# Denominators of the first 256 tokens by a TensorE product, sums of batch 0 for two heads at a time, masks from the identity, and new instruction orders

## The chip, the cores and the metric

One core of a Trainium2 chip runs the whole program. The metric is the device time of one execution in microseconds; a lower number is better. Profiles are of one execution, taken by the hardware profiler.

## The reference

The kernel computes linear attention on polynomial features, followed by a two-layer MLP. The sizes are batch 4, 4 heads, 1088 tokens, head width 32, sketch rank 8, and an MLP of width 128 to 2048 to 128 on 4352 tokens.

```python
def phi(x):
    a = np.einsum('rd,bhsd->bhsr', S1, x)
    b = np.einsum('rd,bhsd->bhsr', S2, x)
    return np.einsum('bhsi,bhsj->bhsij', a, b).reshape(*x.shape[:-1], r * r)
q_p, k_p = phi(q), phi(k)
kv  = np.einsum('bhsf,bhsd->bhfd', k_p, v)
z   = np.sum(k_p, axis=2)
num = np.einsum('bhsf,bhfd->bhsd', q_p, kv)
den = np.einsum('bhsf,bhf->bhs', q_p, z)[..., None] + 1e-06
attn = num / den
x = attn.transpose(0, 2, 1, 3).reshape(B * S, H * D)
h = x @ w_in
out = (h - np.tanh(h)) @ w_out
```

All inputs and outputs are float32.

## The kernel before, in words

The program is a list of operations, each with its engine, its reads and its writes. `ORDER` holds, written out, the order of the operations on each of the five engines; a small planner only walks this order, places waits, and puts filler matmuls (lines 503 and 504, a product of a zero tile with itself) where its own cost figures see TensorE idle, up to the first operation that writes PSUM bank 0. Every engine runs its list strictly in order, and SyncE issues nearly all transfers, also in order.

Per batch, the steps are these. VectorE transposes the raw keys (kT, lines 569 and 573) and queries (qT, line 739). TensorE projects the keys on both sketches (kproj, 582), and VectorE turns the result (kab, 590). The sum over tokens of the key features is a Gram matrix of the two projections (gram, 598); it is masked to its head blocks (zm, 603), multiplied with S2 (ufold, 606), and reduced over heads (uw, 609) to eight more columns of the query projection's weights, w4. The query projection (qproj, 751) then gives, per token and head, the projections a and b and a third vector, whose product with a is the denominator: qab (759), dm (778), den (781), reciprocal rden (784), and qa = a/den (787). The outer products of a and b are qp for the queries (661 or 797) and wk for the keys (629). The sums over tokens of wk times v (642 for batch 0, 711 later) give kv, and the product of kv with the transposed qp gives x directly (693 for batch 0, 820 later).

Batch 0 goes in parts, so that the MLP can begin: tiles 0 and 1 of 128 tokens each alone, then 2 and 3, then 4 to 8. In batch 0, qp is transposed on TensorE (676), copied to qpB (683), and multiplied with kvb, which holds kv of two heads in a block (kvs 648, fold0 651, kvb 530 with pmask). Later batches transpose qp on VectorE (qpT, 803).

The MLP runs in windows of 256 or 512 tokens: L1 (912) multiplies x by a column block of w_in, ScalarE takes the tanh (916), L2 (925) multiplies with w_out. The linear part h @ w_out is folded to one 128 by 128 matrix: w_in is turned (857, 862) and multiplied with w_out (869, wfold), and its product with x is line 897. The weights are cast to bf16 at lines 843 and 847. Results are transposed (osb, 931) and stored (938).

In PSUM, operations of different engines that touch one bank are ordered by waits, also two readers.

Of the kernel before, what the change touches and what calls it, by code (L numbers as in the profile page):

```python
# [52 lines left out]
    ),  # L53
    "scalar": (
# [4 lines left out]
    ),  # L59
    "vector": (  # L60
# [5 lines left out]
    ),  # L66
    "gpsimd": (
        "6 4 5 2 16 20 3 25 7 18 17 19 23 22 79 21 80 24 81 109 106 110 107 108 111 150 152 241 242 247 251 363 365 364 374 370 "
        "508 506 507 517 513 "
    ),  # L70
    "sync": (
# [22 lines left out]
class Program:  # L94
# [46 lines left out]
    def schedule(self):  # L141
# [10 lines left out]
        free = {e: 0 if e == "sync" else BEGIN for e in engines}  # L152
# [10 lines left out]
        while left:  # L163
# [58 lines left out]
            for k in o.kids:  # L222
                seen = o.end + SEEN[k.eng]
# [120 lines left out]
def bass_polysketch_attn__then__act_tanh_shrink_kernel(nc, q, k, v, S1, S2, moe_w_in, moe_w_out, out):  # L344
# [26 lines left out]
    e4 = sb("e4", [4, 4, 4, 8])  # L371
    hmask = sb("hmask", [128, 2])
    pmask = sb("pmask", [128, 2])
    mask = sb("mask", [128, H, R])
# [16 lines left out]
    kvb = sb("kvb", [128, 2, 2, D])  # L391
    qpB = sb("qpB", [128, NT, 2, 128])
# [44 lines left out]
    def load_small():  # L437
        for i, src in enumerate((S1, S2)):
            o = load("scalar", 1024, ("s_raw",), "s", -1000, lambda e, i=i, src=src: e.dma_start(
                out=s_raw[8 * i:8 * i + 8, :], in_=src[:, :]), True)  # L440
            o.lag = -950
# [4 lines left out]
    def load_rows(dst, src, name, b, cuts, prios, first=0):  # L446
        i = b % 2
        for x, (lo, hi) in enumerate(cuts):
            hi = min(hi, S)
            size = 512 * (hi - lo)  # L450
            o = P.op("sync", size / (360 if b else 280), lambda e, lo=lo, hi=hi: e.dma_start(
# [3 lines left out]
            o.lag = 2500 if b == 1 else 0 if b or first else 1100  # L455
            asked.append((o, size))

    def load_keys(prio):
# [9 lines left out]
        for x, (g0, g1, lo, hi) in enumerate(((0, 4, 0, 160), (0, 3, 160, 288), (3, 4, 160, 224))):  # L468
            size = 512 * (g1 - g0) * (hi - lo)
            o = load("sync", size, ("kraw0", min(x, 1)), f"k0{min(x, 1)}", prio, runs(g0, g1, lo, hi), x == 2, 280)  # L470
            if x == 2:
                asked.append((o, size))

    def load_v(b, prio):
        i = b % 2
        src = v[b].rearrange("h (j c) d -> j h c d", j=32)
        for g in range(4):
# [3 lines left out]
                in_=src[:, :, 9 * g:9 * g + n, :].rearrange("j h t d -> j h (t d)")), True, 230)  # L481
            o.lag = 2500 if b == 1 else 0 if b else 900
        asked.append((o, 128 * 128 * 34))

    def load_w_in(prio):
        for x in range(4):
            o = load("sync", 262144, ("w_in_f", x), f"wi{x}", prio, rate=390, fn=lambda e, x=x: e.dma_start(
                out=w_in_f[:, 512 * x:512 * x + 512], in_=moe_w_in[:, 512 * x:512 * x + 512]))

    def load_w_out(prio):  # L490
        for x in range(4):
            load("sync", 262144, ("w_out_f", x), f"wo{x}", prio, rate=300, fn=lambda e, x=x: e.dma_start(
# [8 lines left out]
    def constants():  # L501
# [7 lines left out]
        P.op("gpsimd", 240, lambda e: e.memset(e4[:, :, :, :], 0.0), w=[("e4",)], prio=-999)  # L509
        P.op("gpsimd", 400, select(e4[:, :, :, :], [[0, 4], [-1, 4], [0, 8]], 0), r=[("e4",)], w=[("e4",)], prio=-999)  # L510
        P.op("gpsimd", 240, lambda e: e.memset(e16[:, :, :], 0.0), w=[("e16",)], prio=-998)
        P.op("gpsimd", 400, select(e16[:, :, :], [[0, 16], [-1, 8]], -8), r=[("e16",)], w=[("e16",)], prio=-998)
        P.op("vector", 110, lambda e: e.memset(hmask[:, :], 0.0), w=[("hmask",)], prio=-1000)  # L513
# [3 lines left out]
        P.op("vector", 110, lambda e: e.memset(pmask[:, :], 0.0), w=[("pmask",)], prio=-998)  # L517
        for h in range(2):
            P.op("vector", 110, lambda e, h=h: e.memset(pmask[64 * h:64 * h + 64, h:h + 1], 1.0),
                 w=[("pmask",)], prio=-998)  # L520
        P.op("gpsimd", 240, lambda e: e.memset(dm[:, :, :, R:R + 1], 1e-6), w=[("dme",)], prio=-975)
        for i in range(2):
# [3 lines left out]
            P.op("gpsimd", 240, lambda e, i=i: e.memset(w4[i][:, 24:32], 0.0), w=[("w40", i)], prio=-978 + i)  # L526
# [5 lines left out]
    def sketch():  # L532
# [8 lines left out]
        for h in range(2):  # L541
            scaled(psk[:, :, h, :], ps[:, 5, 0:16].rearrange("p (a i) -> p a i", a=2), hmask[:, h:h + 1], 16,
                   [bank[5], ("hmask",)], [("psk", h)], -899.5, f"psk{h}")
# [3 lines left out]
    def folding():  # L547
        P.op("tensor", 60, lambda e: e.matmul(
            ps[:, 6, 0:32], e4[:, :, :, :].rearrange("p a b c -> p (a b c)"), e4[:, 0, :, :].rearrange("p b c -> p (b c)"),
            start=True, stop=True), r=[("e4",)], w=[bank[6]], prio=-898, mode="s", name="mask", ni=4)  # L550
# [3 lines left out]
        P.op("scalar", act(32), lambda e: e.copy(mask[:, :, :].rearrange("p h i -> p (h i)"), ps[:, 6, 0:32]),  # L554
             r=[bank[6]], w=[("mask",)], prio=-861, name="mask")
        for h in range(H):
            scaled(s2blk[:, h, :], ps[:, 6, 64:96], mask[:, h, 0:1], 32, [bank[6], ("mask",)], [("s2blk", h)], -850, f"s2blk{h}")
# [5 lines left out]
    def keys(b, T, kb, gb, gate=()):  # L563
# [31 lines left out]
        def gram(e):  # L595
# [6 lines left out]
        P.op("tensor", 300, gram, r=[("kab", i, t) for t in range(NT)], w=[bank[gb]], prio=T["gram"], mode="128x32", name=f"gram{b}", ni=36)  # L602
        P.op("vector", dve(32), lambda e: e.tensor_tensor(
            out=zm[i][:, :], in0=ps[:, gb, 0:32], in1=mask[:, :, :].rearrange("p h i -> p (h i)"), op=ALU.mult),
# [30 lines left out]
    def values_first(T, vb, tb, tiled):  # L635


        for m, (t0, t1) in enumerate(tiled):
            def tiles(e, t0=t0, t1=t1, m=m):
                for t in range(t0, t1):  # L640
                    for h in range(H):
                        ins = e.matmul(ps[32 * h:32 * h + 32, tb, 0:64], vx[0][:, h, t, :], wk[:, t, h, :, :],
# [422 lines left out]
```

## Time and profile before

| what | value |
|---|---|
| median of 3 runs | 109.08 us (108.99 to 109.91) |
| the profiled execution | 108.55 us, span 106.7 us |
| TensorE (PE) busy | 96.8 us, 91% of the span |
| ScalarE (ACT) busy | 78.4 us, 73% |
| VectorE (DVE) busy | 61.7 us, 58% |
| GpSimd (POOL) busy | 35.0 us, 33% |
| granted TensorE clock | 1.00 |
| first L1 matmul of the MLP | at 17.26 us |
| num of batch 1 (line 820) | at 39.78 us |

The span is from the first to the last instruction; the time of the execution has 1.85 us more around it. Busy shares are averages over stages with different limits, so they don't say what bounds a stage: in the opening no token can enter the MLP before batch 0's keys, values and first queries have gone through four engines, while at the end only the MLP is left. In timeline lines the columns are start, duration, engine, line, operation, output and inputs, shape and count; in square brackets stands the idle time before it and what ended it. PEld is TensorE's weight load.

### The profile page before, as it was taken

What the parts mean: (1) busy time and instruction counts of PE and PEld (TensorE: products, weight loads), DVE (VectorE), ACT (ScalarE), POOL (GpSimd) and SP (SyncE); (2) the same over time, 40 slices, a digit from 0 to 9 for tenths busy, and PEclk for the clock granted to TensorE, in tenths of its full rate; (3) what the DMA queues carried; (4) which work ended last, traced back from release to release, by engine and by line L of the source; (5) the groups of instructions that cost most, each with busy time, mean ns of one, the idle gap of its engine ahead of it and who ended that gap; (6) DMA issues with size and microseconds to landing.
All of it is one profiled execution on the core that took longest, in us unless ns stands there. A gap on an engine that the chain in (4) does not pass through costs nothing.

```text
span 106.7 us, 2954 instructions
## 1 busy us (share of the span) xinstructions
PE 96.8 (91%) x1246; PEld 50.5 (47%) x1256; DVE 61.7 (58%) x128; ACT 78.4 (73%) x107; POOL 35.0 (33%) x45
## 2 busy tenths in 40 slices
PE   6899985899999969999899999999999999999960
PEld 3357553784656424424544443544344434345540
DVE  2467962999899998689986365927650020200210
ACT  3350874775458974859998797989969999999930
POOL 5737017450491920493930049391000000000000
PEclk9999999999999999999999999999999999999999
DMA  2999999930798300799100410033002324024063
GB/s 38 298 220 289 313 320 259 238 82 0 247 201 233 57 3 0 242 208 262 25 0 7 75 22 0 6 52 47 0 12 37 55 34 68 0 36 62 6 98 49
DMA packets 26509, 11.21 MB, mean 105 GB/s; under 512 B 19072, under 2 KB 24320, under 8 KB 26496
## 3 DMA queue, kind: packets, MB, share of 16 engines
q1 hardware_dynamic: 25920, 10.95, 43.7%
q8 instruction: 10, 0.16, 0.7%
q10 hardware_dynamic: 576, 0.07, 0.4%
q14 instruction: 3, 0.02, 0.1%
HBM read 8.78 MB, written 2.23 MB: 103 GB/s over the span
## 4 chain that ended last, share of the span: by engine, by line
PE 64%; DMA 10%; DVE 9%; ACT 4%; POOL 4%; SPq 3%; issue 3%; POOLq 0%; DVEq 0%
PE ps L925 23%; PE ps L912 23%; DMA w_out_f<-in_moe_w_out_dram 6%; ACT tt L916 4%; DMA vx<-in_v_dram 4%; PE ps L820 4%; PE ps L897 3%; DVE qpT L803 3%; POOL w_out L847 2%; PE ps L751 2%; DVE qp L797 2%; PE ps L582 2%; DVE qab L759 1%; SPq L466 1%; SPq L479 1%
## 5 line engine op out<-in xcount | busy, mean ns | idle before, releaser
L916 ACT ACTIVATE tt<-ps 128x1024 bf16<-128x1024 f32 (+1 forms) x70 | 66.7, 998 | 10.4 <-PE ps L912 8.5
L912 PE MATMUL ps<-xT,w_in 128*128 128x512 bf16 (+1 forms) x154 | 40.9, 346 | 1.6 <-issue 0.8
L925 PE MATMUL ps<-tt,w_out 128*128 128x512 bf16 (+1 forms) x157 | 39.9, 347 | 0.2 <-issue 0.2
L629 POOL TENSOR_TENSOR wk<-kab 128x768 f32<-128x768 f32 (+2 forms) x11 | 15.7, 1425 | 22.3 <-DVE kab L590 21.8
L925 PEld LDWEIGHTS ps<-tt,w_out 128*128 128x128 bf16 x160 | 15.4, 99 | 13.9 <-issue 2.2
L912 PEld LDWEIGHTS ps<-xT,w_in 128*128 128x128 bf16 x160 | 14.3, 97 | 16.0 <-ACT tt L916 4.9
L931 DVE STREAM_TRANSPOSE osb<-ps 128x512 f32<-128x512 f32 (+1 forms) x10 | 6.3, 634 | 22.6 <-PE ps L925 22.6
L797 POOL TENSOR_TENSOR qp<-qa,qab 128x768 f32<-128x768 f32 x6 | 10.3, 1710 | 6.2 <-DVE qa L787 5.9
L803 DVE STREAM_TRANSPOSE qpT<-qp 128x768 f32<-128x768 f32 x9 | 8.4, 959 | 3.1 <-POOL qp L797 3.1
L759 DVE STREAM_TRANSPOSE qab<-ps 128x576 f32<-128x576 f32 (+2 forms) x10 | 6.0, 642 | 3.7 <-PE ps L751 3.7
L739 DVE STREAM_TRANSPOSE qT<-qraw 128x576 f32<-128x576 f32 (+2 forms) x9 | 5.8, 653 | 0.0
L820 PE MATMUL ps<-qpT,kvw 32*32 32x288 f32 (+1 forms) x192 | 4.6, 399 | 0.8 <-DVE qpT L803 0.8
L503 PE MATMUL ps<-wz 128*128 128x512 bf16 x8 | 4.3, 583 | 1.0 <-DVE hmask L513 1.0
L590 DVE STREAM_TRANSPOSE kab<-ps 128x576 f32<-128x576 f32 (+2 forms) x5 | 3.2, 661 | 2.1 <-PE ps L582 2.1
L569 DVE STREAM_TRANSPOSE kT<-kraw 128x576 f32<-128x576 f32 x6 | 4.4, 751 | 0.0
L847 POOL CAST w_out<-w_out_f 128x512 bf16<-128x512 f32 x4 | 2.5, 615 | 5.6 <-DMA w_out_f<-in_moe_w_out_dram 5.2
L830 ACT CAST xT<-ps 128x256 bf16<-128x256 f32 x6 | 2.0, 377 | 3.0 <-PE ps L820 3.0
L797 DVE TENSOR_TENSOR qp<-qa,qab 128x768 f32<-128x768 f32 x3 | 4.2, 1411 | 0.0
L862 ACT COPY w_inT<-ps 128x512 bf16<-128x512 bf16 x4 | 2.3, 586 | 2.3 <-PE ps L857 2.2
L820 PEld LDWEIGHTS ps<-qpT,kvw 32*32 32x32 f32 x192 | 2.4, 103 | 2.8 <-DVE qpT L803 1.2
L711 PEld LDWEIGHTS ps<-wk,vx 128*32 128x32 f32 x216 | 3.2, 110 | 1.2 <-issue 1.2
L843 ACT CAST w_in<-w_in_f 128x512 bf16<-128x512 f32 x2 | 1.2, 618 | 3.3 <-DMA w_in_f<-in_moe_w_in_dram 3.3
(90 smaller groups left out, 94.5 us busy)
## 6 DMA issues: line engine op xcount, KB each, us to landing
vx<-in_v_dram SPq DMA_DIRECT2D x12, 144.0 KB, 4.0
qraw<-in_q_dram SPq DMA_DIRECT2D x4, 288.0 KB, 6.2
w_in_f<-in_moe_w_in_dram SPq DMA_DIRECT2D x4, 256.0 KB, 5.5
w_out_f<-in_moe_w_out_dram SPq DMA_DIRECT2D x4, 256.0 KB, 6.7
out_dram<-osb SPq DMA_DIRECT2D x16, 64.0 KB, 2.0
kraw<-in_k_dram SPq DMA_DIRECT2D x3, 288.0 KB, 5.5
kraw<-in_k_dram SPq DMA_DIRECT2D x3, 256.0 KB, 5.9
qraw<-in_q_dram SPq DMA_DIRECT2D x3, 256.0 KB, 5.5
```

The lines of the kernel that those rows point to most:

```text
L569: P.op("vector", dve(hi - lo), lambda e, lo=lo, hi=hi: e.transpose(out=kT[:, lo:hi], in_=kraw[i][:, lo:hi]), r=cells("kraw", i, lo, min(hi ...
L629: P.op(eng, dve(cols) if eng == "vector" else pool2(cols), lambda e, t0=t0, t1=t1, ap=ap, m=m, ka0=ka0: e.tensor_tensor(out=wk[:, t0:t1, : ...
L739: P.op("vector", dve(hi - lo), lambda e: e.transpose(out=qT[i][:, lo:hi], in_=qraw[i][:, lo:hi]), r=cells("qraw", i, lo, hi), w=cells("qT" ...
L759: P.op("vector", dve(2 * n), lambda e, h=h: e.transpose(out=qab[:, t0:t1, h:h + 2, :].rearrange("p t h x -> p h t x"), in_=ps[:, qb + h:qb ...
L797: P.op(eng, dve(cols) if eng == "vector" else pool2(cols), lambda e, p0=p0, p1=p1, w=w: e.tensor_tensor(out=qp[:, p0:p1, :, :, :].rearrang ...
L803: P.op("vector", dve(cols), lambda e, p0=p0, p1=p1: e.transpose(out=qpT[:, p0:p1, :, :, :].rearrange("p t h y j -> p (t h y j)"), in_=qp[: ...
L820: ins = e.matmul(ps[32 * h:32 * h + 32, nb[g], 0:32 * n], kvw[i][32 * g:32 * g + 32, y, 32 * h:32 * h + 32], qpT[32 * g:32 * g + 32, t0:t0 ...
L847: P.op("gpsimd", 600, lambda e, x=x: e.tensor_copy(w_out[:, 4 * x:4 * x + 4, :], w_out_f[:, 4 * x:4 * x + 4, :]), r=[("w_out_f", x)], w=[( ...
L912: P.op("tensor", pe(n), lambda e, jb=jb + y, y=y, hb=hb: e.matmul(hb[:, n * y:n * y + n], w_in[:, 128 * jb:128 * jb + 128], xT[:, f0:f0 + ...
L916: P.op("scalar", act(q * n), lambda e, un=un, hb=hb, q=q: e.activation(out=tt[:, un, 0:q * n], in_=hb[:, 0:q * n], func=AF.Tanh, scale=-1. ...
L925: P.op("tensor", pe(n), lambda e, jb=jb, un=un, y=y: e.matmul(acc[:, 0:n], w_out[:, jb, :], tt[:, un, n * y:n * y + n], start=(not f0 and ...
L931: P.op("vector", dve(n), lambda e: e.transpose(out=osb[u][:, 0:n], in_=acc[:, 0:n]), r=[ka], w=[("osb", u)], prio=slot0, name=f"osb{w}")
```

## The change

What it does:

- The first two tiles (256 tokens) no longer go through dm, den, rden and qa. Their query projection uses only the plain sketches (w4[1]). The Gram matrix is spread on VectorE (`zx`) and multiplied with the head mask on TensorE (`zfold`), which gives `zden`, a weight that puts each head's denominator on all 32 of the head's output channels. One product with qpB (`zq`) gives the denominators of 256 tokens; ScalarE adds 1e-6 (`dsum`), VectorE takes the reciprocal (`drec`) and multiplies (`x0`).
- The sums of batch 0 multiply two heads at once (128 features against 64 value columns, `pairs`), and the diagonal blocks are copied straight to `kvb`; fold0 and pmask go.
- The mask of head blocks is copied from the identity (`same`) and reduced (`mask`), where before it was a product of `e4` with itself.
- `ORDER` is new for all engines, and the planner's figures of transfers are other ones. One more key product (tile 5) goes to GpSimd.

```diff
+        for g in range(4):
+            P.op("vector", 110, lambda e, g=g: e.tensor_copy(
+                same[32 * g:32 * g + 32, :, :].rearrange("p h i -> p (h i)"), ident[32 * g:32 * g + 32, 32 * g:32 * g + 32]),
...
+        P.op("vector", 110, lambda e: e.tensor_reduce(out=mask[:, :], in_=same[:, :, :], axis=AX.X, op=ALU.add),
...
+            P.op("vector", dve(256), lambda e: e.tensor_tensor(
+                out=zx[:, :, :, :, :].rearrange("p x y i j -> p (x y) i j"),
+                in0=ps[:, gb, 0:32].rearrange("p (h i) -> p h i", i=R)[:, :, :, None].to_broadcast([128, H, R, R]),
+                in1=same[:, :, None, :].to_broadcast([128, H, R, R]), op=ALU.mult),
...
+            def spread(e):
+                for x in range(2):
+                    ins = e.matmul(ps[:, gb, 128 + 64 * x:192 + 64 * x], zx[:, x, :, :, :].rearrange("p y i j -> p (y i j)"),
+                                   mask[:, 2 * x:2 * x + 2, None].to_broadcast([128, 2, D]), start=True, stop=True)
...
+            P.op("scalar", act(128), lambda e: e.copy(
+                zden[:, :, :, :].rearrange("p x y d -> p (x y d)"), ps[:, gb, 128:256]), ...
...
-                        ins = e.matmul(ps[32 * h:32 * h + 32, tb, 0:64], vx[0][:, h, t, :], wk[:, t, h, :, :],
-                                       start=(t == tiled[0][0]), stop=(t == tiled[-1][1] - 1), tile_position=(0, 32 * h))
...
+                if not m:
+                    e.matmul(ps[:, tb, 0:128], wz[:, :], wz[:, :], start=True, stop=False)
+                for t in range(t0, t1):
+                    for x in range(2):
+                        ins = e.matmul(ps[:, tb, 64 * x:64 * x + 64], wk[:, t, 2 * x:2 * x + 2, :, :].rearrange("p h i j -> p (h i j)"),
+                                       vx[0][:, 2 * x:2 * x + 2, t, :], start=False, stop=(t == split[-1][1] - 1 and x == 1))
...
+            P.op("scalar", act(64), lambda e, y=y: e.copy(
+                kvb[64 * y:64 * y + 64, :, y, :], ps[64 * y:64 * y + 64, tb, 0:128].rearrange("p (x y d) -> p x y d", x=2, y=2)[:, :, y, :]),
...
+    def first_pair(t0, T, qb, ab, tb, db, nb, engs):
...
+            P.op("vector", dve(2 * n), lambda e, h=h, x=x: e.transpose(
+                out=qsb[:, u, x, :, :].rearrange("p (t h) f -> p h t f", h=2),
...
+            P.op("scalar", act(32), lambda e, x=x, near=near: e.copy(near, qsb[:, u, x, :, 0:R]),
...
+            P.op("vector", dve(256), lambda e, x=x, near=near: e.tensor_tensor(
+                out=qq[:, x, :, :].rearrange("p t f -> p (t f)").rearrange("p (m i j) -> p m i j", i=R, j=R),
...
+            P.op("tensor", 500, product(zden, db), r=[("zden",)] + ready, w=[bank[db]], prio=T["den"], mode="128x64", name=f"zq.{t0}", ni=8)
+            P.op("scalar", act(256), lambda e: e.activation(out=dsum[:, u, :], in_=ps[:, db, 0:256], func=AF.Copy, bias=1e-6),
...
+            P.op("vector", dve(256), lambda e: e.reciprocal(drec[:, u, :], dsum[:, u, :]), r=[("dsum", u)], w=[("drec", u)], prio=T["den"], name=f"drec{u}")
+            P.op("tensor", 500, product(kvb, nb), r=[("kvb", 0), ("kvb", 1)] + ready, w=[bank[nb]], prio=T["num"], mode="128x64", name=f"num0.{t0}", ni=8)
+            P.op("vector", dve(256), lambda e: e.tensor_tensor(
+                out=xT[:, 128 * t0:128 * t0 + 256], in0=ps[:, nb, 0:256], in1=drec[:, u, :], op=ALU.mult),
...
-    key_products(0, opening, [(0, 2, "gpsimd"), (2, 4, "gpsimd"), (4, 5, "gpsimd")] + [(t, t + 1, "vector") for t in range(5, 9)], 1)
+    key_products(0, opening, [(0, 2, "gpsimd"), (2, 4, "gpsimd"), (4, 5, "gpsimd"), (5, 6, "gpsimd")] + [(t, t + 1, "vector") for t in range(6, 9)], 1)
+    values_first(opening, 3, [(0, 2), (2, 4), (4, 5), (6, 7), (5, 6), (7, 9)])
+    casts(("scalar", "scalar", "gpsimd", "gpsimd"), ())
+    rest = first_pair(0, first, 4, (4, 6), (5, 7), 4, 6, ("scalar", "scalar"))
+    queries(0, 2, 4, then, 4)
+    rest()
```

The orders of the opening in the changed program, read from the built program, with its own line numbers:

- TensorE: fills (4 of 512 columns, 3 of 128), S product (541), fills (512, 512, 128), S2 product (554), kproj of tiles 5 to 8 and 0 to 4 (583), qproj of the first pair (688), gram (599), w_in turn 0, zfold (613), turns of qp (711), ufold (624), qproj of tiles 2 and 3 (830), sums of tiles 0 to 6 (662, 14 products), zq (728), sums of tiles 7 and 8 (4 products), turns of qp of tiles 2 and 3 (755), w_in turn 1, num0 (728), num of tiles 2 and 3 (772), w_in turn 2, three L1 (988), qproj of tiles 4 to 8, ... No fills follow the S2 product.
- VectorE: constants, the two kT, kab of tiles 5 to 8, qT, kab of tiles 0 to 4, two qsb (698), zx (605), two qp (704), qT, zm (620), wk of tile 6 (647), uw (627), wk of tiles 7 and 8, qab of tiles 2 and 3 (838), dm, den, rden, qa, two qp, qT, drec (737), x0 (739), qab of tiles 4 to 8, ...
- ScalarE: psk, s2blk, w4, cast of w_in 0, two qn (702), w_inT 0, zden (618), copy of keys, two qpB, cast of w_in 1, dsum (735), two kvb (669), qpB of tiles 2 and 3, w_inT 1, x of tiles 2 and 3, w_inT 2, tanh, ...
- GpSimd: constants, wk of tile 5, wk of tiles 0 and 1, memsets, wk of tiles 2 and 3, wk of tile 4, casts of w_in 2, w_out 0, w_out 1, w_in 3, w_out 2, w_out 3, ... (before: w_out 1, w_in 2, w_out 2, w_in 3, w_out 0, w_out 3).
- SyncE: keys (the smaller half first), q, w_in 0, v, q, three v, w_out 0, w_in 1, q, w_in 2, w_out 1, w_in 3, w_out 2, w_out 3; then the loads of batches 1 to 3 and the stores interleaved. Two of batch 1's four v loads stand behind the first load of batch 2, which waits for the last x of batch 0, and two of batch 2's four v loads stand behind the first load of batch 3, which waits for x of batch 1.

More of the change, by code (lines that the diff above doesn't have):

```diff
@@ L151, in schedule @@
         head = dict.fromkeys(engines, 0)
-        free = {e: 0 if e == "sync" else BEGIN for e in engines}
+        free = {e: BEGIN for e in engines}
         avail = {e: [] for e in engines}
@@ L222, in schedule @@
             for k in o.kids:
-                seen = o.end + SEEN[k.eng]
+                seen = o.end + SEEN[k.eng] + (300 if dma and k.eng == "gpsimd" else 0)
                 if k.eng == e and not dma:
@@ L370, in bass_polysketch_attn__then__act_tanh_shrink_kernel @@
     e16 = sb("e16", [16, 16, 8])
-    e4 = sb("e4", [4, 4, 4, 8])
     hmask = sb("hmask", [128, 2])
-    pmask = sb("pmask", [128, 2])
-    mask = sb("mask", [128, H, R])
+    same = sb("same", [128, H, R])
+    mask = sb("mask", [128, H])
     s_raw = sb("s_raw", [16, D])
@@ L391, in bass_polysketch_attn__then__act_tanh_shrink_kernel @@
     kvb = sb("kvb", [128, 2, 2, D])
+    zx = sb("zx", [128, 2, 2, R, R])
+    zden = sb("zden", [128, 2, 2, D])
+    dsum = sb("dsum", [128, 1, 256])
+    drec = sb("drec", [128, 1, 256])
+    qsb = sb("qsb", [128, 1, 2, H, 4 * R])
     qpB = sb("qpB", [128, NT, 2, 128])
@@ L454, in load_rows @@
                 after=gated(size))
-            o.lag = 2500 if b == 1 else 0 if b or first else 1100
+            o.lag = 1500 if b == 1 else 300
             asked.append((o, size))
@@ L516, in constants @@
                  w=[("hmask",)], prio=-1000)
[L517 to L520, printed above, removed]
+        P.op("gpsimd", 240, lambda e: e.memset(kvb[:, :, :, :], 0.0), w=[("kvb", 0), ("kvb", 1)], prio=-976)
         P.op("gpsimd", 240, lambda e: e.memset(dm[:, :, :, R:R + 1], 1e-6), w=[("dme",)], prio=-975)
@@ L659, in products_first @@
-    def products_first(T, t, eng, near=None, sb0=None):
-        qf = qa[:, t, :, :] if near is None else near
+                    for x in range(2):
+                        ins = e.matmul(ps[:, tb, 64 * x:64 * x + 64], wk[:, t, 2 * x:2 * x + 2, :, :].rearrange("p h i j -> p (h i j)"),
+                                       vx[0][:, 2 * x:2 * x + 2, t, :], start=False, stop=(t == split[-1][1] - 1 and x == 1))
+                return ins
+            P.op("tensor", 230 * (t1 - t0), pairs, r=[("wz",), ("vx", 0), ("vx0", 0)] + [("wk", t) for t in range(t0, t1)],
+                 w=[bank[tb]], prio=T["sums"] - 0.5 + m * T["sumstep"], mode="s", name=f"pairs.{t0}", ni=8 * (t1 - t0))
@@ L779, in denominators @@
             out=flat(dm)[:, :, 0:R], in0=flat(qab)[:, :, 0:R], in1=flat(qab)[:, :, 2 * R:3 * R], op=ALU.mult),
-            r=[("qab", t) for t in ts], w=[("dm", t) for t in ts], prio=T["den"], after=gate, name=f"dm{b}.{t0}", two=True)
+            r=[("qab", t) for t in ts], w=[("dm", t) for t in ts], prio=T["den"], name=f"dm{b}.{t0}", two=True)
         P.op("vector", dve(8 * m), lambda e: e.tensor_reduce(
@@ L785, in denominators @@
              r=[("den", t) for t in ts], w=[("rden", t) for t in ts], prio=T["den"], name=f"rden{b}.{t0}")
-        spot = flat(qa) if near is None else ps[:, near, 0:8 * m].rearrange("p (m i) -> p m i", i=R)
         P.op("vector", dve(8 * m), lambda e: e.tensor_tensor(
-            out=spot, in0=flat(qab)[:, :, 0:R], in1=flat2(rden)[:, :, None].to_broadcast([128, m, R]), op=ALU.mult),
-            r=[("qab", t) for t in ts] + [("rden", t) for t in ts], w=[("qa", t) for t in ts] + ([] if near is None else [bank[near]]),
-            prio=T["den"], name=f"qa{b}.{t0}", two=near is None)
-        return {} if near is None else {t: spot[:, 4 * (t - t0):4 * (t - t0) + 4, :] for t in ts}
+            out=flat(qa), in0=flat(qab)[:, :, 0:R], in1=flat2(rden)[:, :, None].to_broadcast([128, m, R]), op=ALU.mult),
+            r=[("qab", t) for t in ts] + [("rden", t) for t in ts], w=[("qa", t) for t in ts],
+            prio=T["den"], name=f"qa{b}.{t0}", two=True)
     def products(T, split, b):
@@ L963, in bass_polysketch_attn__then__act_tanh_shrink_kernel @@
                    sums=-850, sumstep=0.1, kvs=-872, kvb=-871)
-    keys(0, opening, ((1, 2), (3, 4)), 7)
+    keys(0, opening, ((1, 2), (3, 4)), 2)
     q_turn(0, 0, -891)
@@ L967, in bass_polysketch_attn__then__act_tanh_shrink_kernel @@
     first = dict(qproj=-892, qab=-892, den=-879, qp=-870, qpT=-869, num=-830, x=-829)
[L968 to L976 removed]
+    then = dict(qproj=-880, qab=-870, den=-820, qp=-819, qpT=0.1, num=2.6, x=-800)
+    key_products(0, opening, [(0, 2, "gpsimd"), (2, 4, "gpsimd"), (4, 5, "gpsimd"), (5, 6, "gpsimd")] + [(t, t + 1, "vector") for t in range(6, 9)], 1)
[4 more added lines that the diff above has]
+    rest()
     denominators(0, 2, 4, then)
[L978 to L979 removed]
     for x in range(4):
[L981 removed]
+        linear_turn((0.6, 0.7, 2.1, 2.2)[x], 0, x, "scalar")
     for t in range(2, 4):
         products_first(then, t, "vector")
[L984 to L986 removed]
+    numerators_first(then, [(2, 4, 5, "scalar")], 7, "scalar")
+    q_turn(0, 2, -800)
     second = dict(qproj=3.1, qab=-798, den=-795, qp=-774, qpT=-773, num=-772, x=-771)
```

127 lines of the change are left out of this document (75 added, 52 removed), and 52 rows, old and new, of the table ORDER.

## The prediction

> **What bounds the kernel now.** I read the chain of waits first, then the windows of busy time, then the timeline of the opening. The chain, in its stretch from 30 to 41 us:
>
> ```profile
> 30.88 1.46 DVE qab L759 x2
> ...
> 34.62 2.06 DVE qp L797
> 36.70 0.98 DVE qpT L803
> ...
> 37.98 1.75 DVE qpT L803 x2
> 39.78 1.55 PE ps L820 x50
> ```
>
> Until the numerators of batch 1 (num1, L820) start at 39.78, the tokens of batch 1 don't exist, and TensorE and ScalarE run out of windows. The chain before that is a VectorE chain. The windows (columns PE, PEld, DVE, ACT, POOL) show how full VectorE is there:
>
> ```profile
> 18.43:39.73 21.30, 19.92 (x268) 12.67 (x270) 20.37 (x38) 15.26 (x18) 10.22 (x8) 1.00 0.56 135
> 80.00:103.00 23.00, 22.87 (x119) 10.99 (x118) 2.23 (x4) 21.74 (x24) 0.00 (x0) 1.00 0.28 43
> ```
>
> VectorE works 20.37 of the 21.30 us from 18.43 to num1; afterwards the MLP fills TensorE and ScalarE. So the end is "start of that VectorE stretch, plus its work, plus a fixed rest". The stretch starts with qab of tiles 4 to 8 (L759). How it gets to 18.43 stands in the timeline:
>
> ```profile
> 15.77 0.27 ACT L699 CAST xT<-ps 128x128 bf16<-128x128 f32 x1
> 16.28 0.62 POOL L843 CAST w_in<-w_in_f 128x512 bf16<-128x512 f32 x1 [0.16 <-POOL w_out L847]
> 17.04 0.38 PE L857 MATMUL ps<-identb,w_in 128*128 128x128 bf16 x4 [0.99 <-POOL w_in L843]
> 17.26 0.49 PE L912 MATMUL ps<-xT,w_in 128*128 128x256 bf16 x3
> 18.43 0.91 DVE L759 STREAM_TRANSPOSE qab<-ps 128x320 f32<-128x320 f32 x2 [1.90 <-PE ps L751]
> 19.37 0.69 DVE L778 TENSOR_TENSOR dm<-qab 128x160 f32<-128x160 f32 x1
> ```
>
> The first x is whole at 16.04; a turn of w_in, held by a cast on GpSimd that itself stood behind a cast of w_out, keeps TensorE to 17.0; L1 starts at 17.26, and qab follows 1.17 us later. VectorE had idled 1.90 us for it. I therefore walk the changed opening to its first L1 and carry the shift to the end.
>
> **The change, part by part.** Prices come from these rows (first the reciprocal at three sizes, then TensorE):
>
> ```profile
> L784 DVE RECIPROCAL rden<-den 128x8 f32<-128x8 f32 x2 | 0.4, 194 | 0.0
> L784 DVE RECIPROCAL rden<-den 128x20 f32<-128x20 f32 x1 | 0.3, 278 | 0.0
> L784 DVE RECIPROCAL rden<-den 128x36 f32<-128x36 f32 x3 | 1.1, 378 | 0.1
> ...
> 11.76 0.30 PEld L651 LDWEIGHTS ps<-ident,kvs 128*128 128x128 f32 x2 [0.30 <-ACT kvs L648]
> 9.91 1.23 PE L642 MATMUL ps<-wk,vx 128*32 128x64 f32 x72
> 8.80 0.58 PE L503 MATMUL ps<-wz 128*128 128x512 bf16 x1
> 11.07 0.39 PE L503 MATMUL ps<-wz 128*128 128x512 bf16 x1
> ```
>
> *Head.* S lands as before (its product at 4.36). Behind it the new order has fills of 512, 512 and 128 columns instead of two of 128: a 512 goes every 0.40 us there (7.80 to 8.20), so +0.6, and kproj starts at 6.1 instead of 5.51. With the smaller half of the keys first, kab comes at 6.85 (6.40 before), then qT 0.40 and the second kab 0.52: 8.2.
>
> *First pair.* qproj now needs no folded sketch (w4[1], not w4[0]) and lies under the second kab. On VectorE follow: two qsb of 128 elements, 0.30 each (428 ns at 256 and 496 at 320 give 1 ns an element); zx 0.40 and two qp 0.40 each, as the 256-element products from PSUM; qT 0.40: from 8.35 to 10.55. qn, w_inT, zden and the copy of the keys (0.17 to 0.59 each) run on ScalarE beside this; zfold is two fp32 products of the kind of ufold (0.58), about 1.0 us, so zden ends at 10.7, and zm, which the bank makes wait for zden, ends at 10.9. ufold 0.6, uw: 11.8. Only now can the second qproj go (12.0 to 12.4), and behind it in TensorE's queue stand the sums of batch 0, which waited for nothing else (GpSimd's key products end near 11.7).
>
> *Sums.* Before, 36 tile products of 32 columns took 1.23 us (L642). Now 18 products load 128x128 fp32 weights in two passes each. The fold's two loads (L651: 188 ns each, 0.30 together) start 0.11 apart, the transposes of qp go every 0.13: I take 2 x 0.112 = 0.224 us a product, 4.0 us in all. Bounds: 0.07 (the tile price, 1.23/18) and 0.43 (ufold at 8.4 us: two loads of 337 ns, 0.215 apart). Fourteen of them stand ahead of zq: 12.5 + 3.1 = 15.65, zq 0.55 (L693 with 256 columns), dsum 0.38 on ScalarE: 16.6. ScalarE's w_in cast ahead of dsum waits for a transfer that I place near 12 (2.2 MB asked for up to it, against 2.4 MB landed by 12.9 before): 4 us of cover.
>
> *Reciprocal.* Before, one took 8 to 36 elements a partition. Now drec takes 256 in one instruction. The three rows give (378 - 194)/28 = 6.6 ns an element: 0.19 + 248 x 0.0066 = 1.83 us. Lower bound: 0.42, an ordinary 256-element operation; upper 1.9 (7.0 ns, the first two rows). I take 1.83, since three sizes lie on one line. VectorE reaches it at about 15.7 (wk, qab, dm to qa, two qp, qT: 3.9 us from 11.8) and waits for dsum: 16.6 to 18.45. The rest of the sums, four turns, a w_in turn and num0 (0.9 + 0.5 + 0.4 + 0.55) end at 18.4, beside it. x0 0.42: 18.9, first L1 at 18.95 instead of 17.26, +1.7.
>
> [...]
>
> *What is given back.* The casts are reordered by landing and end near 18.0 rather than 19.90; dm at 19.37 took 689 ns beside them, where 64 elements take 222 and 288 alone 460, so about 330: -0.36. VectorE's waits for TensorE later in the stretch (0.30 before zm, 0.23 before qab of batch 1) shrink when VectorE is the later one: I take half, -0.25. The VectorE list from qab to num1 is otherwise the same 38 instructions. The constants (e4, pmask gone, same and mask new) lie before 4 us, where VectorE idled 2.3 us for the keys; without that cover they cost 0.5. The masks' product and fold0 with its two kvb activations leave TensorE and ScalarE where both had idle time: nothing.
>
> *SP.* Loads and outputs are interleaved now. Two of batch 1's four v transfers stand behind a batch 2 load that waits for batch 0's last x (26 us); at up to 6.7 us to landing they arrive near 33, and sums1 is 0.85 us of MLP work later in TensorE's order than its 32.80: no cost, up to 1 if the queue is full. Batch 2's are a rival below.
>
> **Sum.** +1.7 - 0.36 - 0.25 = +1.1 us. The profiled execution took 108.55 (span 106.7 and 1.85 around it), 109.65 then; the median of the runs is 109.08, 0.53 higher, so 110.2.
>
> **Rivals.** (1) *Sums at the tile price*, chance 0.17: TensorE hides the loads, drec starts at 15.7 and x0 ends at 17.95; L1 at 18.0, +0.74 - 0.61: 109.2. For it: L642 does the same multiplications in 1.23. Against: L651.
> (2) *Faster*, 0.13: the same, and drec is an ordinary operation of 0.42. x0 then ends at 16.55, L1 at 16.6: -0.66 - 0.36, and up to 0.6 more if S lands earlier, so that the fills cost nothing: 107.9. It decides if drec lasts under 0.6 us. Against: the three L784 rows.
> (3) *TensorE stays slow*, 0.15: the 512-column fill took 0.58 up to 8.80 and 0.39 at 11.07, after fills that closed every gap from 6.65 on. The new order has no fill after the S2 product. If TensorE meets the sums at the slow price, ten instead of nineteen products fit into the 4.2 us that it needed before to speed up (4.95 to 9.2): zq 1.95 later, 112.1. The profile's granted clock stays 1.00 in both states. [...]
> (4) *Late v*, 0.05: batch 2's last two v transfers are issued after batch 1's x (42 us), the last as eighth; eight took 4.6 us, landing 3.6 to 6.7: 50 to 53 against sums2 at 51.47. From 5.2 us to landing on it stalls TensorE, on average by 1: 111.2.
>
> **Numbers.** Forecast 0.50, its own range 109.2 to 111.3. About 1% is what a measurement can tell here. Slower by more: 0.30 of the forecast, all of (3) and (4), 0.01 of (1): 0.51. Within 1%: 0.20, 0.13 of (1) and 0.03 of (2): 0.36. Faster: 0.10 and 0.03: 0.13. The range, 108.0 to 112.2, takes in (1), (3), (4) and the upper part of (2).
>
> **What would show it.** Right: L662 lasting 4 us with 0.22 between products, L737 at 1.8 us, first L1 near 18.9, num1 (L896) near 40.9. Wrong: L737 under 0.6; sums within 1.5 us; L1 before 17.3; or num1 that doesn't move with L1, which would mean that VectorE didn't bound the stretch.

## The result, and the profile after

The changed kernel takes 116.15 us (median of 4 runs, 115.22 to 117.39) against 109.06 (108.99 to 109.91, 4 runs of the kernel before): 1.0622 times as long, interval 1.0551 to 1.0692. The prediction had 110.2, at most 112.2. Its profiled execution took 116.43 us with a span of 114.1; before it was 108.55 and 106.7. So 7.9 us are to be found in one pair of traces. Here and below a time is the median of all runs of a kernel, while a ratio compares only the runs within 1.5% of each kernel's fastest one, so the two need not agree to the last digit.

The chain of waits of the kernel after (start, duration, engine, tile, line):

```profile
12.19 5.98 PE ps L662 x28
18.17 1.05 PE ps L728 x4
...
24.85 0.64 PE ps L988 x3
...
26.18 0.93 DVE qab L838 x2
...
46.92 1.61 PE ps L896 x50
...
53.88 5.19 DMA vx<-in_v_dram
```

First L1 (L988; 24.64 in the timeline below) starts 7.38 later than the 17.26 of before, the copy of the queries' projections (qab) starts at 26.18 instead of 18.43 (+7.75), the numerators of batch 1 (num1, L896) at 46.92 instead of 39.78 (+7.14), and the span ends 7.4 later. All of the loss lies ahead of the first L1, and the chain there is TensorE. Its largest piece is L662, the pair sums: 28 passes, that is 14 products, in 5.98 us. In the trace the passes start 0.213 us apart, two a product: 0.43 where the prediction took 0.224. The timeline shows the stretch:

```profile
11.99 6.18 PE L662 MATMUL ps<-vx,wk 128*128 128x64 f32 x28
18.10 1.12 PE L728 MATMUL ps<-qpB,zden 128*64 128x256 f32 x4
19.15 1.97 PE L662 MATMUL ps<-vx,wk 128*128 128x64 f32 x8
19.27 0.38 ACT L735 ACTIVATE dsum<-ps 128x256 f32<-128x256 f32 x1 [7.45 <-PE ps L728]
19.69 1.75 DVE L737 RECIPROCAL drec<-dsum 128x256 f32<-128x256 f32 x1 [4.23 <-ACT dsum L735]
...
22.34 1.12 PE L728 MATMUL ps<-qpB,kvb 128*64 128x256 f32 x4
23.57 0.42 DVE L739 TENSOR_TENSOR xT<-ps,drec 128x256 bf16<-128x256 f32 x1 [2.13 <-PE ps L728]
24.64 0.85 PE L988 MATMUL ps<-xT,w_in 128*128 128x256 bf16 x3
```

Everything behind the sums is dear too: zq and num0 (L728) take 1.12 us each, where the prediction had 0.55. The reciprocal lasts 1.75 us, and x0 (L739) still waits 2.13 us for num0 after it. The summary by windows (columns PE, PEld, DVE, ACT, POOL, then the granted clock) gives no hint why:

```profile
12.00:18.00 6.00, 6.00 (x29) 5.98 (x29) 3.18 (x10) 0.00 (x0) 3.77 (x6) 1.00 1.09 332
```

TensorE and its weight loads are busy for the whole 6 us, at a clock of 1.00. The trace holds one thing more, its records of TensorE's clock, with the entries 1.00 and 0.50; no view prints them one by one, and every start of full clock below is read from them. The first entry of 1.00 (full clock) begins at 9.22 us in the kernel before and at 25.49 in the kernel after; the 1.00 in the rows ahead of that is no record but the absence of one. That TensorE ran at half of the full clock there is read from its products: the same ones take about twice as long ahead of that entry as behind it. A pass of the pair sums starts every 0.213 us here, ahead of the entry, and every 0.112 us in a_burst below, behind it.

### The profile page after: what moved, and what is told of

Its sections match the earlier page's. It is cut to its first block, busy times and chain, and to the rows that moved or that the text cites. A ratio compares the mean times of both kernels' runs of the same rounds, so it can differ in the third digit from the quotient of the medians.

```text
span 114.1 us, 2913 instructions
## 1 busy us (share of the span) xinstructions
PE 105.7 (93%) x1226; PEld 58.1 (51%) x1237; DVE 64.8 (57%) x128; ACT 78.9 (69%) x109; POOL 35.9 (31%) x45
## 4 chain that ended last, share of the span: by engine, by line
PE 69%; DVE 13%; DMA 8%; SPq 5%; issue 2%; ACT 1%; DVEq 0%
PE ps L988 19%; PE ps L1001 19%; PE ps L662 7%; DMA vx<-in_v_dram 5%; PE ps L896 4%; DMA kraw<-in_k_dram 3%; PE ps L973 3%; SPq L484 3%; DVE qpT L879 2%; PE ps L830 2%; DVE qab L838 2%; PE ps L790 2%; PE ps L755 2%; PE ps L583 2%; PE ps L728 2%
## 5 line engine op out<-in xcount | busy, mean ns | idle before, releaser
L988 PE MATMUL ps<-xT,w_in 128*128 128x512 bf16 (+1 forms) x153 | 41.0, 350 | 1.1 <-issue 1.0
L1001 PE MATMUL ps<-tt,w_out 128*128 128x512 bf16 (+1 forms) x157 | 39.3, 347 | 0.1
L988 PEld LDWEIGHTS ps<-xT,w_in 128*128 128x128 bf16 x160 | 14.3, 99 | 17.0 <-ACT tt L992 5.3
L873 POOL TENSOR_TENSOR qp<-qa,qab 128x768 f32<-128x768 f32 x6 | 11.0, 1838 | 6.2 <-DVE qa L864 6.0
L662 PEld LDWEIGHTS ps<-vx,wk 128*128 128x128 f32 x36 | 7.9, 331 | 0.8 <-issue 0.8
L662 PE MATMUL ps<-vx,wk 128*128 128x64 f32 x36 | 8.2, 423 | 0.0
L896 PE MATMUL ps<-qpT,kvw 32*32 32x288 f32 (+1 forms) x192 | 4.6, 399 | 0.5 <-DVE qpT L879 0.5
L674 POOL TENSOR_TENSOR qp<-qa,qab 128x256 f32<-128x256 f32 x2 | 1.5, 774 | 10.9 <-DVE qa L864 10.8
L873 DVE TENSOR_TENSOR qp<-qa,qab 128x768 f32<-128x768 f32 x3 | 4.9, 1643 | 0.0
L737 DVE RECIPROCAL drec<-dsum 128x256 f32<-128x256 f32 x1 | 1.8, 1753 | 4.2 <-ACT dsum L735 4.2
L790 PE MATMUL ps<-wk,vx 128*32 128x64 f32 x216 | 3.6, 220 | 0.5 <-DMA vx<-in_v_dram 0.5
L790 PEld LDWEIGHTS ps<-wk,vx 128*32 128x32 f32 x216 | 3.2, 110 | 1.8 <-DMA vx<-in_v_dram 1.0
```

The costliest lines, as they stand in the source:

```text
L662: ins = e.matmul(ps[:, tb, 64 * x:64 * x + 64], wk[:, t, 2 * x:2 * x + 2, :, :].rearrange("p h i j -> p (h i j)"), vx[0][:, 2 * x:2 * x + ...
L790: ins = e.matmul(ps[32 * h:32 * h + 32, vb, 0:64], vx[i][:, h, t, :], wk[:, t, h, :, :], start=(t == 0), stop=(t == NT - 1), tile_position ...
L873: P.op(eng, dve(cols) if eng == "vector" else pool2(cols), lambda e, p0=p0, p1=p1, w=w: e.tensor_tensor(out=qp[:, p0:p1, :, :, :].rearrang ...
L896: ins = e.matmul(ps[32 * h:32 * h + 32, nb[g], 0:32 * n], kvw[i][32 * g:32 * g + 32, y, 32 * h:32 * h + 32], qpT[32 * g:32 * g + 32, t0:t0 ...
L988: P.op("tensor", pe(n), lambda e, jb=jb + y, y=y, hb=hb: e.matmul(hb[:, n * y:n * y + n], w_in[:, 128 * jb:128 * jb + 128], xT[:, f0:f0 + ...
L1001: P.op("tensor", pe(n), lambda e, jb=jb, un=un, y=y: e.matmul(acc[:, 0:n], w_out[:, jb, :], tt[:, un, n * y:n * y + n], start=(not f0 and ...
```

## The experiments

Two theories. A: TensorE is at half clock until work without gaps brings it to full clock, the new order left out the fills that did so, and the sums met the half clock. B: 0.43 us is simply what a product with 128 columns of fp32 weights costs.

**The kernel before without its fills (b_nofill).**

```diff
-    P.fill_stops = {o for o in P.ops if o.eng == "tensor" and o in P.wrote.get(bank[FB], ())}
+    P.fill_stops = {o for o in P.ops if o.name == "kproj0.0"}
```

> The kernel before, with the fills (products of zeros that only keep TensorE busy) ended at kproj, where the changed kernel ends them too; nothing else differs. Theory A (TensorE has a slow and a fast state that the granted clock doesn't show, and only work without gaps brings it into the fast one; the new order left out the fills that did so): the 36 tile products of L642 take about 2.4 us instead of 1.23, the turns of w_in 0.21 us a piece instead of 0.13, the first L1 starts near 20 instead of 17.26, and the kernel takes 111 to 112.5 us. Theory B (the price of 0.43 us for a product of the sums belongs to a load of 128 fp32 columns, and has nothing to do with the fills): tiles 1.23, L1 17.3 or a little earlier, 109.1 us.

Measured: 109.28 us, ratio 1.003 (0.9985 to 1.0074). A's price was right and its time was wrong:

```profile
10.65 2.15 PE L642 MATMUL ps<-wk,vx 128*32 128x64 f32 x72
...
17.22 0.38 PE L857 MATMUL ps<-identb,w_in 128*128 128x128 bf16 x4
17.44 0.49 PE L912 MATMUL ps<-xT,w_in 128*128 128x256 bf16 x3
```

The tile products take 2.15 us instead of 1.23, but full clock begins at 13.35, behind them. What was lost by then disappears in a wait: the turn of w_in at 17.22 now comes after its cast on GpSimd, which is done at 16.70, and the 0.99 us for which it waited before are gone. The old order survives the loss of its fills. So their absence alone isn't the whole cause, and something in the new work must keep TensorE at half clock for 12 us longer.

**A burst ahead of the sums (a_burst).**

```diff
+            for _ in range(32):
+                e.matmul(ps[:, 3, 256:512], wz, <wz, 256 columns>, start=True, stop=True)
+    ... placed directly ahead of pairs.0
```

> The changed kernel with one burst of 32 products of zeros, 256 columns each, on TensorE directly ahead of the sums of batch 0. By A their interval falls from 0.21 to 0.107 us somewhere within the burst, which lasts 4 to 6 us; behind it a product of the sums costs 0.22 to 0.25 us instead of 0.43, zq, the turns and num0 go at half of their price too, the first L1 starts at 22.5 to 24 instead of 24.85 although the burst stands on the path, and the kernel takes 114 to 115.5 us. By B the sums keep 0.43 us a product, the burst is added whole: first L1 near 29.5, 120 to 121 us.

Measured: 115.48 us, ratio 1.0602 (1.0525 to 1.0679). The timeline:

```profile
11.85 5.94 PE L1122 MATMUL ps<-wz 128*128 128x256 bf16 x32
...
17.68 3.29 PE L670 MATMUL ps<-vx,wk 128*128 128x64 f32 x28
...
24.52 0.49 PE L996 MATMUL ps<-xT,w_in 128*128 128x256 bf16 x3
```

Full clock begins at 16.53, and then 14 products of the sums take 3.29 us, a pass every 0.112 us: the same instructions as in the kernel after, at half the price. B falls. The kernel does 5.9 us of useless work on the path of the opening and is no slower for it. L1 comes 0.5 us later than A's bound, since the burst is near the long end of A's range.

**The same products in the gaps (a_fill).** Fourteen of the 256-column products in front of operations for which TensorE waited anyway:

```diff
+    fills("qproj0.0", 2, 0)
+    fills("gram0", 2, 0)
+    fills("zfold", 3)
+    fills("qt0.0.0", 1)
+    fills("qt0.0.1", 1)
+    fills("ufold0", 2)
+    fills("qproj0.2", 3)
```

> The changed kernel with 14 products of zeros, 256 columns each, spread over TensorE's gaps from kproj to the sums (2 ahead of kproj's successor qproj, 2 ahead of the Gram product, 3 ahead of zfold, 1 and 1 ahead of the turns of qp, 2 ahead of ufold, 3 ahead of the second qproj). By A TensorE is fast from about 10 or 11 us on: 14 products of the sums in 3.2 to 3.6 us instead of 6.2, zq 0.55 us instead of 1.05, first L1 at 18.9 to 20 instead of 24.85, num1 (L896 in the kernel after) at 40.9 to 42, 110 to 111.5 us; the reciprocal drec (1.75 us) then ends last ahead of x0. By B the sums stay at 6.2 us and only the other products gain: L1 near 23.5, 114.5 to 116 us.

Measured: 110.68 us, ratio 1.0086 (1.0028 to 1.0144): 5.5 us of the loss come back, by the ratios 86% of it. The timeline:

```profile
11.93 3.29 PE L670 MATMUL ps<-vx,wk 128*128 128x64 f32 x28
...
16.26 1.75 DVE L745 RECIPROCAL drec<-dsum 128x256 f32<-128x256 f32 x1 [1.15 <-ACT dsum L743]
...
18.77 0.49 PE L996 MATMUL ps<-xT,w_in 128*128 128x256 bf16 x3
...
40.69 1.55 PE L904 MATMUL ps<-qpT,kvw 32*32 32x288 f32 x64 [0.48 <-DVE qpT L887]
```

Full clock begins at 9.39. This is the run in which the forecast's own assumption on TensorE holds: L1 at 18.77 (forecast 18.9), num1 at 40.69 (40.9). The reciprocal ends at 18.01 and num0 at 18.08 by the chain, level with each other.

**The old sums in the new order (a_tiles).** The 18 products for two heads are replaced by the 36 tile products, the copy to kvs and fold0 of the kernel before; no fills are added.

```diff
-                    for x in range(2):
-                        ins = e.matmul(ps[:, tb, 64 * x:64 * x + 64], <wk of two heads, 128 columns>, <v of two heads>, ...)
+                    for h in range(H):
+                        ins = e.matmul(ps[32 * h:32 * h + 32, tb, 0:64], vx[0][:, h, t, :], wk[:, t, h, :, :], ...)
```

> The changed kernel with the sums of batch 0 done as before (four tile products of 32 columns for each of nine tiles, a copy on ScalarE and one fold product) in place of the 18 products for two heads; order and fills as in the changed kernel. By A TensorE is slow here too: 36 tile products take about 2.4 us (28 of them 1.9) instead of 1.23, the turns of qp stay at 0.21 us a piece; drec starts near 15.5 and no longer waits long for the sums, the first L1 starts near 20 to 20.5, about 111.5 us. By B the 36 tile products take 1.23 us, L1 near 19, about 110.2 us. By both the sums are what the change lost most by: 4 to 5 of its 7 us come back.

Measured: 109.76 us, ratio 1.0037 (0.9985 to 1.0089), below what either theory gave.

```profile
12.13 1.72 PE L666 MATMUL ps<-wk,vx 128*32 128x64 f32 x56
13.78 1.12 PE L741 MATMUL ps<-qpB,zden 128*64 128x256 f32 x4
```

The products are dear (28 in 1.72 us, as A had it), but full clock begins at 15.37, not at 25.49. So with the same fills and nearly the same start, full clock came 3.24 us after the first of the tile products (12.13) and 13.5 us after the first of the pair sums (11.99). Theory A in its first form, "work without gaps", falls: from 11.45 on the kernel after has no gap either. Of the two guesses that replace it, A1 says that fp32 work with 128 columns of weights, or fp32 work at all, doesn't count; A2 that what counts is the share of the time in which columns stream through the array.

**Thin bf16 products as the burst (a_thin16).**

```diff
+        for x in range(50):
+            e.matmul(ps[:, 3, 256:288], (identb, wz)[x % 2], wz[:, 0:32], start=True, stop=True)
```

> The changed kernel with a burst of 50 bf16 products directly ahead of the sums, each with a fresh load of 128 columns of weights and only 32 moving columns, so that TensorE has no gap and yet streams columns in a small part of the time, as in the sums. Theory A1 (time without gaps brings TensorE to its full clock, but fp32 work doesn't count): full clock within the burst, as with the 256-column burst, the sums at 0.23 us a product, 115 to 116 us. Theory A2 (what counts is the share of time in which columns stream through the array): the burst passes without a change of clock, lasts 5.4 us or more, the sums stay at 0.43, 121 to 122 us.

Measured: 117.19 us, ratio 1.0725 (1.0637 to 1.0814), and no answer. A bf16 product with a fresh load of 128 columns takes only 0.027 us here, so the burst was over in 1.35 us instead of 5.4, too short for either theory. The sums behind it took 6.18 us again.

**Wide and narrow fp32 products as the burst (a_wide32, a_narrow32).** Both put 14 products of `ident` ahead of the sums and differ in the moving columns alone, 256 and 64; each was run twice:

```diff
+        for x in range(14):
+            e.matmul(ps[:, 3, 256:512], ident, <ident twice, 256 columns>, start=True, stop=True)    # a_wide32
+            e.matmul(ps[:, 3, 256:320], ident, ident[:, 0:64], start=True, stop=True)                # a_narrow32
```

> The changed kernel with a burst of 14 fp32 products directly ahead of the sums, 128 columns of weights and 256 moving columns each (two passes a product). A1 (fp32 work doesn't count): no change of clock, the burst lasts 6 us, the sums stay at 0.43 us a product, 121 to 122 us. A2 (the share of streaming time counts): full clock some 4 to 5 us into the burst, sums at 0.23, 115 to 116 us.

> The kernel with the burst of 14 fp32 products ahead of the sums, 128 columns of weights each, with one difference: 64 moving columns instead of 256, as in the sums. By A2 (the share of the time in which columns stream through the array, taken over a stretch of some 3.4 us) nothing raises the clock in some 12 us of work without a gap: the burst lasts 6 us, the sums behind it 0.43 us a product, first L1 near 31, 122 us. If work without gaps is enough and the changed kernel only had its work too late or cut at the wrong place, full clock comes within the burst or early in the sums, and the kernel takes 116 to 118 us.

Measured: a_wide32 118.16 us, ratio 1.0814 (1.0728 to 1.0900); a_narrow32 120.87 us, ratio 1.105 (1.0942 to 1.1158). The timeline of a_wide32, then of a_narrow32:

```profile
12.14 9.17 PE L1120 MATMUL ps<-ident 128*128 128x256 f32 x28
...
21.20 3.29 PE L670 MATMUL ps<-vx,wk 128*128 128x64 f32 x28
```

```profile
12.15 6.23 PE L1120 MATMUL ps<-ident 128*128 128x64 f32 x28
...
18.28 6.18 PE L670 MATMUL ps<-vx,wk 128*128 128x64 f32 x28
24.39 1.12 PE L736 MATMUL ps<-qpB,zden 128*64 128x256 f32 x4
...
28.62 1.12 PE L736 MATMUL ps<-qpB,kvb 128*64 128x256 f32 x4
29.53 0.99 PE L780 MATMUL ps<-qpB,kvb 128*64 128x256 f32 x4
```

Wide: full clock at 17.96, within the burst, and cheap sums. Its passes start 0.427 us apart before that and 0.216 after, where I had taken 0.213 and 0.107 from the bf16 fills, so the burst is 3 us longer than expected and the time lies between A2's figure and A1's. Narrow: some 12 us of narrow products without a gap (12.15 to 24.39), and full clock only at 30.31, behind turns of 128 columns and the 256-column products of num0 and num (L780). The kind of number and the load are the same in both; the moving columns alone differ. A1 falls; A2 isn't refuted. For the stretch of some 3.4 us in A2 the runs have the 3.41 us for which full clock lasted in a_thin16 (4.40 to 7.81); that a share is taken over such a stretch was not shown. The share can be estimated from these rows: if 256 fp32 columns go every 0.427 us at half clock, 64 take at most a quarter of it, 0.107 us, of the 0.213 from one narrow pass to the next, so half of the time at most. The tile products of a_tiles start in fours, on four blocks of columns of the array, every 0.107 us: at that price they stream all the time, and full clock came 3.24 us after the first of them, with zq behind them. So by this estimate 12 us of products that stream for at most half of the time passed without full clock, and 3.24 us of products that stream all the time ended with it, if zq is counted among these. Whether the columns made the difference or something that goes with them, such as the smaller share of time that goes into weight loads, isn't settled.

**Fills and old sums together (a_fill_tiles).** The edits of a_fill and a_tiles in one kernel.

> The changed kernel with both parts: the products of zeros spread over the gaps, and the sums by 36 tile products as before. What is then left of the change is the new way to the denominators (Gram product, spread product, one reciprocal of 256) and the new orders. By the theory of the slow state: tiles at 1.23 us, zq starts near 13.1, drec ends near 16.5 to 17.3, first L1 at 17.5 to 18, num1 (L896 in the kernel after) near 39.8 to 40.1, 108.9 to 109.4 us, no difference from before that can be told. If the denominators' new way costs something that the earlier runs hid, num1 stays at 40.2 or later and the time at 109.7.

Measured: 109.2 us, ratio 0.9982 (0.9944 to 1.0021): no difference from before. The steps in its profiled execution (109.57 us) come later than expected: zq at 13.91, L1 at 18.96, num1 at 40.89. Its second half of the keys was transposed 0.7 us later than in a_fill, full clock began at 11.01, and drec ended at 18.38. By num1 that is the second expectation, by the time the first; which of them holds stays open. Its sums in the timeline, then its chain of waits:

```profile
12.99 0.99 PE L666 MATMUL ps<-wk,vx 128*32 128x64 f32 x56
...
14.88 0.43 PE L666 MATMUL ps<-wk,vx 128*32 128x64 f32 x16
```

```profile
16.74 1.64 DVE drec L750
...
18.48 0.44 DVE xT L752
```

Here x0 (L752) waits for the reciprocal; num0, a group of 0.65 us that started at 16.92, was done at 17.6. With the old sums, drec is what ends last. Against a_fill (1.0086) the ratio is 1% lower. The pair sums take 4.39 us of TensorE even at full clock (3.29 and 1.10) against 1.42 (0.99 and 0.43); that the 1% is theirs is likely but not shown by this pair of traces, whose times are level (109.57 and 109.63).

**SP's order (a_fill_sp).** In a_fill, two of batch 2's loads of v go ahead of a load that waits:

```diff
-        "259 290 218 381 260 385 382 379 380 383 261 350 ...
+        "259 290 218 260 261 381 385 382 379 380 383 350 ...
```

> The changed kernel with the products of zeros spread over the gaps (110.7 us), and in SP's queue two of batch 2's loads of v (260, 261) moved ahead of a load that waits (381). If the late v holds TensorE at the sums of batch 2 (the chain of waits goes through the landing of v at 52.6 us), the wait goes and the end comes up to 0.3 us earlier against num1: from num1 to the end 67.1 us become 66.8 to 67.0, 110.3 to 110.6 us. If the late v is worth the 1 us that the prediction gave it as a rival, 109.7 us.

Measured: 111.47 us, ratio 1.0158 (1.0058 to 1.0259), and inconclusive as a time. Full clock began at 13.04 in its profiled execution, not at 9.39, so num1 came at 42.57. From num1 to the end of the span it is 67.0 us against 67.1 in a_fill, and the wait for v is gone from the sums of batch 2; that is the least of the 0.1 to 0.3 us expected, inside the noise.

**The casts alone (b_casts).** The kernel before with one line of the change, GpSimd's casts with all of w_in ahead of w_out:

```diff
-  ... 24 81 109 106 110 107 108 111 150 ...
+  ... 24 81 106 107 108 109 110 111 150 ...
```

> The kernel before with one part of the change alone: GpSimd's six casts of the weights in the order 106 to 111 (all of w_in ahead of w_out) in place of 109, 106, 110, 107, 108, 111. If the first L1 at 17.26 hangs on the cast of w_in that stood behind a cast of w_out (the turn waited 0.99 us for it), L1 starts near 16.2 to 16.4, num1 (L820) near 39.0, and the kernel takes 107.9 to 108.3 us. If something else then ends as late (the numerators' copy, the turn ahead), 108.6 to 109.1.

Measured: 107.8 us, ratio 0.9858 (0.9818 to 0.9897): faster than both kernels. The timeline:

```profile
12.10 0.61 POOL L843 CAST w_in<-w_in_f 128x512 bf16<-128x512 f32 x1 [1.89 <-DMA w_in_f<-in_moe_w_in_dram]
...
15.30 1.40 PE L693 MATMUL ps<-qpB,kvb 128*64 128x128 f32 x8
16.63 0.40 PE L857 MATMUL ps<-identb,w_in 128*128 128x128 bf16 x4
16.86 0.49 PE L912 MATMUL ps<-xT,w_in 128*128 128x256 bf16 x3
```

The cast that was done at 16.9 is done at 12.7, and the turn (L857 at 16.63) waits for nothing. L1 gains only 0.40 of the 0.9 to 1.1 us expected, since num0 (L693) waits in its middle for a copy of qpB on VectorE; num1 starts at 39.39 (39.78 before) and the profiled execution takes 107.98 us (108.55). The medians differ by more (1.5 us), of which the rest isn't explained by these two traces. Beside a_fill_tiles (0.9982, L1 at 18.96) this run says one thing more: even with full clock at the old sums, the new way to the denominators in the new order is no gain over the old way with its casts in a better order.

## Why the prediction was wrong

**The step that failed** is the price of the sums: "I take 2 x 0.112 = 0.224 us a product". Both rows behind it, the fold's loads at 11.76 and the turns of qp, were taken from a stretch of the trace that had full clock since 9.22, and the sum carried that price to a new order in which TensorE had not reached full clock; only rival 3 allowed for that. The upper bound that stood beside it, 0.43 from ufold at 8.4, was the price at half clock, and it was the one that came. Its excess over the forecast was 3.1 us up to zq (6.18 for 3.1); zq itself, the last four products, the turns, num0 and the w_in turn ahead of it were forecast from rows of the same late stretch, and most of them took about twice their price. The products for the tokens of tiles 2 and 3 (num, L772) and another w_in turn, which stand between num0 and L1 in TensorE's order, are not in the sum at all; by the chains they took 1.39 us in the kernel after and 0.85 in a_fill.

**Rival 3 had the mechanism and missed the size.** It said that TensorE would meet the sums at half clock, with the granted clock at 1.00 in both cases, and gave 112.1. Its failed step is that ten products "fit into the 4.2 us that it needed before to speed up", after which the rest would go at full clock. TensorE stayed at half clock through all 18 products and on to 25.49. The runs put that on the kind of product: with tile products in their place full clock came at 15.37 (a_tiles), and a burst with 256 moving columns had it 5.82 us after its start (a_wide32, 17.96 less 12.14), one with 64 and the pair sums behind it not in 12 us (a_narrow32). The rival's zq was to be 1.95 us later than 15.65; it was 2.45 later, and L1 was 5.7 later than the forecast. The 4.2 us counted time without a gap, and time without a gap was not enough.

**What held.** With full clock at the sums (a_fill) the forecast's steps came within 0.3 us (L1 18.77 for 18.9, num1 40.69 for 40.9) and the time within 0.5 (110.68 for 110.2). That L1 came so close is in part luck: x0 was done 0.35 us earlier than forecast (18.55 for 18.9), and num and the turn of w_in behind it, which the sum left out, took half of that back. The head was better than forecast: S's product came at 3.51 (4.36 before), kproj at 5.41 instead of 6.1, the sums began at 11.99 instead of 12.5; the fills of 512 columns cost nothing that shows. The reciprocal took 1.75 us (forecast 1.83). The reciprocal's place on the path did not come about in the kernel after, where num0 ended 2.0 us later than drec, but does in a_fill_tiles. What is given back between qab and num1 was 0.61 us (7.75 less 7.14), as much as the two terms 0.36 and 0.25 together, but only the first came as costed: dm took 0.32 us, where it took 0.69 beside the casts. VectorE's waits for TensorE didn't shrink: they are 0.52 us in that stretch (0.23 ahead of osb, 0.29 ahead of qab of batch 1) where they were 0.53, so the agreement of the second term is luck. The claim that VectorE carries the shift of L1 to the end holds with +7.75 at qab, +7.14 at num1 and +7.4 at the end. The w_in cast ahead of dsum was covered, as costed: dsum waited 7.45 us for zq and not for it.

**The other rivals.** Rival 1 (tile price) and rival 2 (reciprocal under 0.6 us) are refuted by L662 and L737. Rival 4 (late v) happened: v lands at 59.06, and TensorE's load for sums2 (L790) waits 1.0 us for it. But the sums of batch 2 aren't as urgent as the rival had them: from num1 to the end of the span it is 67.2 us (114.1 less 46.92) against 66.9 before (106.7 less 39.78), so 0.3 us are lost, and a_fill_sp puts 0.1 on it.

## What to carry to other kernels

Before a price is taken from a row, look at what clock TensorE had there, by the duration of one known instruction early and late and not by the granted clock of the summary; carry the price over only if the changed order reaches the same clock by then. Work without a gap did not by itself bring TensorE to full clock here: narrow products behind 128-column fp32 loads ran for 12 us without it (a_narrow32), and fourteen wide products of zeros in gaps that exist anyway were worth 5.5 us (a_fill). In an opening where weights arrive by DMA, order the casts by who is waited for first, since here one cast, queued behind another that waited for its transfer, held TensorE for 0.99 us.

## What the runs showed of the hardware

- In the profiled executions full clock lasted 98.99 us in the kernel before (9.22 to 108.21), 95.57 in a_burst, a_fill_tiles and a_fill_sp, 92.16 in b_nofill and 88.75 in the kernel after (25.49 to 114.24). Each of these lengths is 3.41 or 3.42 us from the next; why, no run shows.
- In the kernel after, TensorE ran nothing but pair sums and zq from 11.99 to 20.92, without a gap, and stayed at half clock until 25.49.
- Full clock can come late with nearly the same products ahead of it: the same opening with fills had it at 9.39 in one kernel (a_fill) and at 13.04 in another that differs only in later transfers (a_fill_sp). TensorE was busy for 3.31 of the 3.41 us up to 9.39 in the first, and for 3.23 of the 3.41 us up to 9.63 in the second; why only the first had full clock then isn't settled.
- It ended early in one run: in a_thin16 full clock began at 4.40 and ended at 7.81, with a gap of 1.21 us in between (TensorE was busy for 1.94 of these 3.41 us), and came back only at 24.88.
- A pass with 128 columns of fp32 weights and 64 moving columns took 0.213 us at half clock (kernel after) and 0.112 at full (a_burst); a bf16 product with a fresh load of 128 columns and 32 moving ones took 0.027 us at half clock (a_thin16). Halving the number of products by loading 128 columns of fp32 weights for each in place of 32 was therefore no saving: at full clock 18 pair products took 4.39 us (a_fill) and 36 tile products 1.42 (a_fill_tiles).
